# A GEGLU and Fourier-mixing kernel: moving the side work, stream requests and bank fills of a seven-product matrix multiplication

## The chip, the cores and the metric

The kernel runs on one core of a Trainium2 chip. The metric is the device time of one execution in microseconds (us). A time is given as the median of three runs with the lowest and the highest of them. Engine names are those of the profile: PE is TensorE (matrix products), PEld its weight loads, DVE is VectorE, ACT is ScalarE, POOL is GpSimd, SP is SyncE. POOL and SP here only start DMA transfers.

## The reference

The input is 2048 tokens of 640 numbers, all in fp32. One branch is a Fourier mixing by two dense matrices, the other a gated feed-forward layer with 1728 hidden numbers; a sigmoid gate per token mixes them.

```python
def _A_ref(x, dft_seq_re, dft_seq_im, dft_hid_re, dft_hid_im):
    a = jnp.einsum("bsd,ed->bse", x, dft_hid_re)
    b = jnp.einsum("bsd,ed->bse", x, dft_hid_im)
    y = jnp.einsum("ts,bse->bte", dft_seq_re, a) - jnp.einsum("ts,bse->bte", dft_seq_im, b)
    return y

def _B_ref(x, w_gate, w_up, w_down):
    return (_gelu(x @ w_gate) * (x @ w_up)) @ w_down

g = _sigmoid((x * gate_w).sum(-1, keepdims=True))
return g * a + (1 - g) * b
```

## The kernel before

**Numbers.** [...] One product is three matmuls into the same PSUM bank (`mm3`, L101 to L103): high by high, high by low, low by high. A high part is a copy on ACT (L82), a low part a difference on DVE (L85), so DVE's low part always waits for ACT's high part. A bank holds 128 x 512 fp32 and there are eight banks.

**Stages.** First the tokens and the first weights are loaded and summed; then the loop over hidden blocks `for f in range(1, NF)` (L1353, NF = 13) computes gate and up projections; behind it, from some 366 us of the span on, come the Fourier mixing and the down projection.

**The hidden-block loop.** Each f is a block of 128 hidden numbers; the tokens are two pairs, tp 0 and 1. `gate_up` (L596) makes one f for one token pair by a Strassen-Winograd form: seven block products instead of eight, with sums of weight blocks on the left (S1 to S4) and sums of token blocks on the right (T1 to T4). Bank X takes A11, then S2 T2, then S3 T3, then u5 x1, each added to what is there. So between them the running value must be taken out of X: the sum into s1 (L629, DVE), the copy s2 (L149, ACT), the sum into s5 (L667, DVE). Bank Z takes S1 T1, then D and S4. `gate_up` is a generator; its pieces are the steps 0 to 6 (rows) of the loop below, each taken for tp 0 and then tp 1.

From f = 3 on (PAIRED) blocks go in couples: the first of a couple (3, 5, 7, 9, 11) also computes products shared by both blocks, again by seven products, in `together` and `together_up`. From f = 5 on (THIRD) there is a third such product, S1 times T1 of two blocks and two token pairs, in `together_s` (L554). Its parts:

- The right operands T1, T2, T3 are streams: made once in f = 4 by `sums_across` (its functions `s123`, with loads `loads_s` ahead of them), stored in DRAM, and fetched again for each couple by `load_across` (L1319; the transfer is L1321 on POOL's queue) into tiles `xs`. T4 (`s4th`) stays on the core.
- The left operands are weight sums in tiles `wt` (`make_third`, L260). They are loaded and summed in the second block of the couple before.
- The results for the couple's second block f + 1 are parked in tiles `sz` (L579 and L588 are the last sums into them) and put back into two fresh banks pZ by `unpark` (L591, the ACT copies L594).

The other streams of a couple, `xq` and `xu`, go by the same `load_across`. Results of a block go to DRAM with `keep` (L448, POOL): `hA` four times a block, as soon as DVE has made them, and `hT` for some blocks. The wait of a store holds up whatever stands behind it in POOL's queue.

**Weights.** `load_w` (L213) and `load_up` (L228) ask for a block's weights on SP (tiles `wa`, `wb`, `wq`, `wu`); `make_w` (L290) and `make_up` give back lists of small sums, high and low parts with a cost each. In the list, `ws` are S1 to S4 of one block, `wd` is D, `wq` holds the left sums shared by a couple.

**What sets the order.** The loop stands in `in_order(PE, ACT, DVE, POOL)` (L1352): on these engines instructions run in the order in which they are written. SP's requests go in their queue's order, each when its tile is free. The lists of small sums are put into one queue, `fills`, at the start of an f; `fill` (L1326) takes from its head whenever PE work has been written, in proportion to that work, and all that is left is written at the end of the f. So the list's order decides which sums stand ahead of which other DVE and ACT work.

In a block the loop reads:

```python
for step in range(8 if not kind else 7):
    if third and step == 6:
        unpark(f + 1, zs, parks)
    for tp, w in enumerate(work):
        run(w)
```

`kind` is 1 for the first of a couple, 2 for the second, 0 before the couples; `third` is true for first blocks from f = 5 on. After the rows of a step come the requests that the diff shows.

Of the kernel before, what the change touches and what calls it, by code (L numbers as in the profile page):

```python
# [9 lines left out]
F32 = mybir.dt.float32  # L10
F32R = mybir.dt.float32r
# [3 lines left out]
P = 128  # L15
# [7 lines left out]
NF = F // P  # L23
# [5 lines left out]
PAIRED = 3  # L29
THIRD = 5  # L30
# [7 lines left out]
def kernel(  # L38
# [36 lines left out]
    def mtile(dt, name):  # L75
        return pool.tile([P, T], dt, tag="m", name=name, bufs=15)
# [4 lines left out]
    def high(hi, raw):  # L81
        nc.scalar.activation(hi, raw, AF.Copy)  # L82
# [120 lines left out]
    def wsmall(dt, name):  # L203
        return pool.tile([P, 2, P], dt, tag="w", name=name, bufs=6)

    def pair_of(f):


        return 0 if f < PAIRED or f >= NF else 2 - (f - PAIRED + 1) % 2
# [3 lines left out]
    def load_w(f):  # L213


        if f >= NF:
            return
        ra, rb = slot(F32, [P, 8, P], f"wa{f}r"), wsmall(F32, f"wb{f}")
        nc.sync.dma_start(ra, wf[f - 1, :, :8])
        nc.sync.dma_start(rb, wf[f - 1, :, 8:])  # L220
        rq = None
        if pair_of(f) == 1:
            rq = slot(F32, [P, 8, P], f"wq{f}r")
            nc.sync.dma_start(rq[:, 0:2], wf[f, :, 0:2])
            nc.sync.dma_start(rq[:, 2], wf[f, :, 4])
        wraw[f] = ra, rb, rq
# [30 lines left out]

        return W, [(112, across), (0, high_u), (78, low_u)]

    def make_third(f):  # L260

        W = {}
        raw, own = ([mtile(dt, f"wt{f}{n}").rearrange("p (b c) -> p b c", c=P) for n in names] for dt, names in ((F32, "ab"), (F32R, "hl")))
        last = wsmall(F32R, f"wt{f}")
        a, b = raw
        for v, c in ((a, 8), (b, 2)):
            for q in range(2):
                nc.sync.dma_start(v[:, 2 * q : 2 * q + 2], wf[f - q, :, c : c + 2])

        def sums():  # L270
            tt(a, a, b, op=ALU.add)
            high(last[:, 0], a[:, 1])

        def across():
            tt(b[:, 0], a[:, 0], a[:, 1], op=ALU.add)
            tt(b[:, 2], a[:, 2], a[:, 0], op=ALU.subtract)
            tt(b[:, 1], b[:, 0], a[:, 2], op=ALU.subtract)
            tt(b[:, 3], a[:, 3], b[:, 1], op=ALU.subtract)
            high(own[0], b)

        def lows():
            low(last[:, 0], last[:, 1], a[:, 1])
            low(*own, b)
            W["A22p"] = last[:, 0], last[:, 1]
            for k in range(4):
                W[f"S{k + 1}p"] = at(own, k)

        return W, [(69, sums), (112, across), (97, lows)]

    def make_w(f):  # L290

# [187 lines left out]
    hid, todo = {}, deque()  # L479
# [624 lines left out]
    W0, load_part, parts, first_strassen = load_first()  # L1104
    Bs = []
    B, tiles, load, piece, tsum, his, lows = load_x(0)
# [28 lines left out]
    with in_order(ACT, DVE, PE):  # L1135
# [5 lines left out]
        for d in range(ND):  # L1141
# [3 lines left out]
            if d == 0:  # L1145
                a, b = halves
# [37 lines left out]
        B, tiles, load, piece, tsum, his, lows = load_x(1)  # L1184
# [62 lines left out]
        W, work = make_w(1)  # L1247
        sums, high_a, sums2, high_c, low_a, diff, low_c = (do for _, do in work)
# [103 lines left out]
    with in_order(PE, ACT, DVE, POOL):  # L1352
        for f in range(1, NF):  # L1353
            kind = pair_of(f)
            if f == PAIRED:
                loadu()
                fills.extend([*t4, *u123[:3], *late_work, *u123[3:], *u4])
            fills.extend(todo)
            todo.clear()
            if kind == 1:  # L1360
                up, work = make_up(f, load_up(f))
                fills.extend(work)
            if f == PAIRED - 1:
                loadp()
                fills.extend(t123)
            if f == THIRD - 1:
                loads_s()
                fills.extend(s123)
            if f + 1 < NF:
                nxt, work = make_w(f + 1)  # L1370
                if kind != 1 or f == PAIRED:
                    fills.extend(work)
            if kind == 1 and f > PAIRED:
                fills.extend(work)
            if pair_of(f + 1) == 1 and f + 1 >= THIRD:
                ws, work = make_third(f + 1)
                fills.extend(work)
            if f == NF - 1:
                for k in range(2):
                    fetch_xn(k)  # L1380
                    load_c(k)

                def made():
                    sums_made.pop(0)()

                for k in range(2):
                    fills.extend([(126, partial(split_xa, k)), (122, made), (245, partial(split_c, k))])
                fills.extend([(126, partial(split_xa, 2)), (122, made)])
            state.update(pe=0, done=0, all=sum(c for c, _ in fills), pe_all=2450 if not kind else (2994, 1768)[kind - 1] if f < THIRD else (3198, 1496)[kind - 1])
            s5 = pair(F32, f"s5{f}")  # L1390
            xs = {}
            work = [gate_up(f, W, Bs[tp], tp, s5[:, tp], s1t, xs, s4, zs) for tp in range(2)]
            more = together(f, W, Tp, s1t, xs) if kind == 1 else iter(())
            more_up = together_up(f, W, up, s4) if kind == 1 else iter(())
            store_left()
            if f == 2:
                k = len(fills) // 2
                rest = [fills.pop() for _ in range(len(fills) - k)]
                fills.extend([*sum_h0(0), *sum_h0(1), *reversed(rest)])
                state["all"] = sum(c for c, _ in fills)  # L1400
            third = kind == 1 and f >= THIRD
            if third:
                parks.clear()
                more_s = together_s(f, W, ws, s5, zs, parks)
            for k in range(4):
                run(more)
                if third and k in (1, 3):
                    load_across(f, "xs", Ts, kepts, k)
            for step in range(8 if not kind else 7):
                if third and step == 6:  # L1410
                    unpark(f + 1, zs, parks)
                for tp, w in enumerate(work):
                    run(w)
                    if third:
                        if step == 0:
                            run(more_s if not tp else more)
                        if (step, tp) == (0, 1):
                            load_across(f, "xu", Tu, keptu, 1)
                            run(more_s)
                            load_across(f, "xu", Tu, keptu, 2)  # L1420
                            run(more)
                            run(more_s)
                            run(more)
                            run(more_s)
                            load_across(f, "xu", Tu, keptu, 3)
                        elif (step, tp) == (2, 0):
                            run(more_s)
                            run(more_s)
                        elif (step, tp) == (3, 0):
                            run(more_s)  # L1430
                    elif (step, tp) in ((0, 1), (1, 1)):
                        run(more)
                        if step == 0:
                            run(more)
                    if (2, 0) < (step, tp) < (6, 0):
                        run(more_up)
                if step < 2 and kind == 1 and PAIRED < f < THIRD:
                    for k in ((1,), (2, 3))[step]:
                        load_across(f, "xu", Tu, keptu, k)
                if step == 4 and pair_of(f + 1) == 1 and f + 1 > PAIRED:  # L1440
                    for k in (1, 2, 3):
                        load_across(f + 1, "xq", Tp, keptp, k)
                if step == 6 and pair_of(f + 1) == 1 and f + 1 >= THIRD:
                    load_across(f + 1, "xs", Ts, kepts, 2)
                if step == 5 and f == THIRD - 1:
                    for _, do in s4th:
                        do()
                if step == 5:
                    load_w(f + 2)
                if f == NF - 1 and step == 3:  # L1450
                    fetch_xn(2)
                if f == NF - 1 and step == 5:
                    load_c(2)
                    fetch_xn(3)
            for v in (more, more_up) + ((more_s,) if third else ()):
                next(v, None)
            while fills:
                fills.popleft()[1]()
            W = nxt
# [59 lines left out]
    for i, (j, ri, b, sp) in enumerate(cseq):  # L1519
# [31 lines left out]
        n = f"{j}{ri}"  # L1551
# [358 lines left out]
```

## Time and profile before

| | us |
|---|---|
| median of 3 runs | 1039.74 (1038.99 to 1040.75) |
| the profiled execution's own time | 1040.26 |
| its span (first to last instruction) | 1038.5 |
| DVE busy in the span | 838.8 (81%) |
| ACT busy in the span | 510.6 (49%) |

The profile is of one execution. Busy time is the time in which an engine runs an instruction. A row of a timeline reads: start in us from the span's start, duration, engine, line, operation, output tile <- input tiles (buffer numbers left out), shape; in square brackets how long the engine had stood idle just before and what ended that. A row of a group of waits reads: who waited <- for whom, then total us, times, longest us. The end of a matmul is modelled, so the idle time that stands beside one is a little short of what a wait really costs.

### The profile page before, as it was taken

The page shows a single profiled execution, that of the slowest core. Times are in us where ns is not written, and L with a number is a line of the kernel's source. Part 1 is how long each engine was busy: PE and PEld are TensorE (multiplying, and loading weights), DVE is VectorE, ACT ScalarE, POOL GpSimd, SP SyncE. Part 2 cuts the span into 40 slices and gives each one's busy share as a digit, 9 for nine tenths or more (in the row PEclk, how much of TensorE's full clock was granted, in tenths as well). Part 3 has the DMA queues.
Part 4 walks back from the last instruction along what each step waited for, and adds up shares of the span by engine and source line. Part 5 has one row for each costly group of instructions (what it writes and reads, how often), then busy time and mean ns, then how long its engine had stood idle before and what let it go on. Part 6 is the DMA issues. An engine that isn't in the chain of part 4 may idle for free.

```text
span 1038.5 us, 13424 instructions
## 1 busy us (share of the span) xinstructions
PE 1018.9 (98%) x4477; PEld 834.6 (80%) x4477; DVE 838.8 (81%) x1197; ACT 510.6 (49%) x666; POOL 188.5 (18%) x330
## 2 busy tenths in 40 slices
PE   9999989999999999999999999999999999999998
PEld 7888767777777878888888888888888888888887
DVE  8987783859584798986978697769798997997796
ACT  6644453545454575442444344334636737655340
POOL 1221230323130011023103310310111010111112
PEclk9999998999999999999999999999999999999999
DMA  9466674676666898679768976989989998997856
GB/s 352 150 218 216 216 244 158 218 241 216 233 218 228 275 285 215 208 266 392 256 204 305 395 241 199 358 306 302 330 315 359 351 393 332 349 372 219 264 161 92
DMA packets 98598, 276.51 MB, mean 266 GB/s; under 512 B 13088, under 2 KB 25504, under 8 KB 98528
## 3 DMA queue, kind: packets, MB, share of 16 engines
q1 hardware_dynamic: 69216, 182.88, 50.4%
q0 software_dynamic: 29024, 92.57, 28.1%
q8 instruction: 35, 0.57, 0.2%
q14 instruction: 35, 0.29, 0.1%
q10 hardware_dynamic: 288, 0.20, 0.1%
HBM read 201.13 MB, written 66.60 MB: 258 GB/s over the span
## 4 chain that ended last, share of the span: by engine, by line
PE 88%; DVE 4%; issue 3%; DMA 2%; ACT 1%; POOL 1%; POOLq 0%; DVEq 0%; ACTq 0%
PE pX L103 5%; PE pX L102 5%; PE pX L101 5%; PE pZ L101 3%; PE pZ L102 3%; PE pZ L103 3%; PE pL L102 3%; PE pL L103 3%; PE pL L101 3%; DMA xs<-xs 2%; PE pV L102 2%; PE pV L103 2%; PE pV L101 2%; PE pY L102 1%; PE pR L102 1%
## 5 line engine op out<-in xcount | busy, mean ns | idle before, releaser
L82 ACT ACTIVATE ch<-csa 128x1024 fp32r<-128x1024 f32 x32 | 34.0, 1062 | 79.2 <-DVE csa L886 67.0
L448 POOL DMA_DIRECT2D hA<-s x48 | 26.1, 545 | 175.2 <-DVE s L679 154.6
L82 ACT ACTIVATE ch<-cra 128x1024 fp32r<-128x1024 f32 x32 | 33.9, 1059 | 45.3 <-DVE cl L85 14.3
L85 DVE TENSOR_TENSOR cl<-cra,ch 128x1024 fp32r<-128x1024 f32 x32 | 39.1, 1222 | 18.5 <-ACT ch L82 16.3
L85 DVE TENSOR_TENSOR cl<-crb,ch 128x1024 fp32r<-128x1024 f32 x32 | 39.1, 1223 | 14.8 <-ACT ch L82 14.7
L102 PE MATMUL pL<-cl,xah 128*128 128x512 f32 x128 | 49.8, 389 | 0.0
L103 PE MATMUL pL<-ch,xal 128*128 128x512 f32 x128 | 49.8, 389 | 0.0
L101 PE MATMUL pL<-ch,xah 128*128 128x512 f32 x128 | 48.8, 389 | 0.0
L82 ACT ACTIVATE ch<-crb 128x1024 fp32r<-128x1024 f32 x32 | 33.8, 1056 | 28.4 <-DVE cl L85 10.8
L85 DVE TENSOR_TENSOR cl<-csa,ch 128x1024 fp32r<-128x1024 f32 x32 | 39.1, 1222 | 9.3 <-ACT ch L82 8.2
L85 DVE TENSOR_TENSOR cl<-csb,ch 128x1024 fp32r<-128x1024 f32 x32 | 39.2, 1225 | 4.2 <-ACT ch L82 3.2
L82 ACT ACTIVATE ch<-csb 128x1024 fp32r<-128x1024 f32 x32 | 34.0, 1062 | 12.8 <-DVE csb L889 4.6
L149 ACT ACTIVATE s<-pX 128x512 f32<-128x512 f32 x41 | 23.9, 593 | 32.8 <-PE pX L103 32.1
L1510 POOL DMA_DIRECT2D uA<-c x8 | 4.3, 540 | 168.9 <-DVE c L1622 168.3
L102 PEld LDWEIGHTS pL<-cl,xah 128*128 128x128 f32 x128 | 24.0, 188 | 5.0
L101 PEld LDWEIGHTS pL<-ch,xah 128*128 128x128 f32 x128 | 24.0, 188 | 5.0
L103 PEld LDWEIGHTS pL<-ch,xal 128*128 128x128 f32 x128 | 24.0, 188 | 5.0
L82 ACT ACTIVATE kh<-kw 128x1024 fp32r<-128x1024 f32 x24 | 25.5, 1063 | 5.0 <-PE kL L102 3.1
L667 DVE TENSOR_TENSOR s<-s,pX 128x512 f32<-128x512 f32 x24 | 16.3, 684 | 13.9 <-PE pX L103 13.9
L102 PE MATMUL pX<-cl,xah 128*128 128x512 f32 x64 | 25.0, 391 | 0.7 <-DVE cl L85 0.7
L85 DVE TENSOR_TENSOR kl<-kw,kh 128x1024 fp32r<-128x1024 f32 x18 | 22.0, 1222 | 4.4 <-ACT kh L82 4.4
L103 PE MATMUL pX<-ch,xal 128*128 128x512 f32 x64 | 25.0, 391 | 0.0
(3785 smaller groups left out, 3519.9 us busy)
## 6 DMA issues: line engine op xcount, KB each, us to landing
cra<-in_ct SPq DMA_DIRECT2D x64, 512.0 KB, 5.2
crb<-in_ct SPq DMA_DIRECT2D x64, 512.0 KB, 5.9
kr<-hA SPq DMA_DIRECT2D x36, 512.0 KB, 7.8
hA<-s POOLq DMA_DIRECT2D x48, 256.0 KB, 3.1
ux<-uA SPq DMA_DIRECT2D x24, 512.0 KB, 7.8
ux<-uT SPq DMA_DIRECT2D x16, 512.0 KB, 6.4
hT<-s POOLq DMA_DIRECT2D x24, 256.0 KB, 4.6
xq<-xp POOLq DMA_DIRECT2D x12, 512.0 KB, 5.2
```

What stands on the lines that cost most here:

```text
L82: nc.scalar.activation(hi, raw, AF.Copy)
L85: nc.vector.tensor_tensor(lo, raw, hi.bitcast(F32), op=ALU.subtract)
L101: nc.tensor.matmul(ps, lh, rh, start=first, stop=False, skip_group_check=True)
L102: nc.tensor.matmul(ps, lh, rl, start=False, stop=False, skip_group_check=True)
L103: nc.tensor.matmul(ps, ll, rh, start=False, stop=last, skip_group_check=True)
L149: nc.scalar.activation(m, src, AF.Copy)
L448: nc.gpsimd.dma_start(to[:, i], src)
L667: tt(s5, s5, X, op=ALU.add)
L1510: nc.gpsimd.dma_start(to[:, i], src)
```

## The change

Five things move; no product is added or removed.

- `make_third` is split: `load_third(f)` asks for the raw weights one block earlier, and the sums, high parts and low parts of `wt` are woven into the head of the list of f's second block: first the sums, after two sums of `make_w` the differences, and so on, instead of at the end of the list.
- T2 of the next couple is asked for after step 5, not step 6, which puts the request ahead of the four `hA` stores.
- `unpark` comes ahead of step 5, not 6.
- `loads_s` and the first three functions of `s123` move from the start of f = 4 to step 4 of f = 3; `s4th` is put off to f = 5's side work.
- In the first block of a couple from f = 5 on, the weights of the second block are asked for and summed from step 1 of that block, not from step 5 of the block before.

```diff
--- before.py
+++ after.py
@@ -257,25 +257,33 @@
 
         return W, [(112, across), (0, high_u), (78, low_u)]
 
-    def make_third(f):
-
-        W = {}
-        raw, own = ([mtile(dt, f"wt{f}{n}").rearrange("p (b c) -> p b c", c=P) for n in names] for dt, names in ((F32, "ab"), (F32R, "hl")))
-        last = wsmall(F32R, f"wt{f}")
-        a, b = raw
+    traw = {}
+
+    def load_third(f):
+
+        traw[f] = a, b = [mtile(F32, f"wt{f}{n}").rearrange("p (b c) -> p b c", c=P) for n in "ab"]
         for v, c in ((a, 8), (b, 2)):
             for q in range(2):
                 nc.sync.dma_start(v[:, 2 * q : 2 * q + 2], wf[f - q, :, c : c + 2])
 
+    def make_third(f):
+
+        W = {}
+        a, b = traw.pop(f)
+        own = [mtile(F32R, f"wt{f}{n}").rearrange("p (b c) -> p b c", c=P) for n in "hl"]
+        last = wsmall(F32R, f"wt{f}")
+
         def sums():
             tt(a, a, b, op=ALU.add)
-            high(last[:, 0], a[:, 1])
 
         def across():
             tt(b[:, 0], a[:, 0], a[:, 1], op=ALU.add)
             tt(b[:, 2], a[:, 2], a[:, 0], op=ALU.subtract)
             tt(b[:, 1], b[:, 0], a[:, 2], op=ALU.subtract)
             tt(b[:, 3], a[:, 3], b[:, 1], op=ALU.subtract)
+
+        def highs():
+            high(last[:, 0], a[:, 1])
             high(own[0], b)
 
         def lows():
@@ -285,7 +293,7 @@
             for k in range(4):
                 W[f"S{k + 1}p"] = at(own, k)
 
-        return W, [(69, sums), (112, across), (97, lows)]
+        return W, [(69, sums), (112, across), (0, highs), (97, lows)]
 
     def make_w(f):
 
@@ -1364,16 +1372,16 @@
                 loadp()
                 fills.extend(t123)
             if f == THIRD - 1:
-                loads_s()
-                fills.extend(s123)
-            if f + 1 < NF:
+                fills.extend(s123[3:])
+            third = kind == 1 and f >= THIRD
+            if f + 1 < NF and not third:
                 nxt, work = make_w(f + 1)
+                if pair_of(f + 1) == 1 and f + 1 >= THIRD:
+                    ws, (sums, across, highs, lows) = make_third(f + 1)
+                    work = [sums, *work[:2], across, *work[2:4], highs, work[4], lows, *work[5:]]
                 if kind != 1 or f == PAIRED:
                     fills.extend(work)
-            if kind == 1 and f > PAIRED:
-                fills.extend(work)
-            if pair_of(f + 1) == 1 and f + 1 >= THIRD:
-                ws, work = make_third(f + 1)
+            if kind == 1 and PAIRED < f < THIRD:
                 fills.extend(work)
             if f == NF - 1:
                 for k in range(2):
@@ -1398,7 +1406,6 @@
                 rest = [fills.pop() for _ in range(len(fills) - k)]
                 fills.extend([*sum_h0(0), *sum_h0(1), *reversed(rest)])
                 state["all"] = sum(c for c, _ in fills)
-            third = kind == 1 and f >= THIRD
             if third:
                 parks.clear()
                 more_s = together_s(f, W, ws, s5, zs, parks)
@@ -1407,7 +1414,7 @@
                 if third and k in (1, 3):
                     load_across(f, "xs", Ts, kepts, k)
             for step in range(8 if not kind else 7):
-                if third and step == 6:
+                if third and step == 5:
                     unpark(f + 1, zs, parks)
                 for tp, w in enumerate(work):
                     run(w)
@@ -1440,12 +1447,21 @@
                 if step == 4 and pair_of(f + 1) == 1 and f + 1 > PAIRED:
                     for k in (1, 2, 3):
                         load_across(f + 1, "xq", Tp, keptp, k)
-                if step == 6 and pair_of(f + 1) == 1 and f + 1 >= THIRD:
+                if step == 5 and pair_of(f + 1) == 1 and f + 1 >= THIRD:
                     load_across(f + 1, "xs", Ts, kepts, 2)
-                if step == 5 and f == THIRD - 1:
-                    for _, do in s4th:
-                        do()
-                if step == 5:
+                if f == THIRD - 2 and step == 4:
+                    loads_s()
+                    fills.extend(s123[:3])
+                if f == THIRD - 1 and step == 5:
+                    todo.extend(s4th)
+                if step == 5 and THIRD <= f + 2 < NF and pair_of(f + 2) == 1:
+                    load_third(f + 2)
+                if third and step == 1:
+                    load_w(f + 1)
+                    nxt, parts = make_w(f + 1)
+                    fills.extend(parts)
+                    state["all"] += sum(c for c, _ in parts)
+                if step == 5 and not (f + 2 >= THIRD and pair_of(f + 2) == 2):
                     load_w(f + 2)
                 if f == NF - 1 and step == 3:
                     fetch_xn(2)
```

Lines behind `make_third` stand 8 higher in the changed kernel: L667 becomes L675, L629 L637, L448 L456, L1321 L1329.

Three places show how the order moves. The first is POOL's queue at the end of f = 6, before the change: the three `xq` streams and `xs72` (T2) for f = 7, the stores `hA` of f = 6, and `hT`.

```order
L1321 DMA xq73_1830<-xp3_569 128x1024
L448 DMA hA02_67<-s26_0_1797 128x512
L448 DMA hA02_67<-s1510_1563 128x512
L448 DMA hA12_73<-s26_1_1810 128x512
L448 DMA hA12_73<-s1511_1479 128x512
L1321 DMA xs72_1866<-xs2_574 128x1024
L448 DMA hT02_79<-s25_0_1582 128x512
L448 DMA hT02_79<-s55_1461 128x512
```

After it:

```order
L1329 DMA xq73_1830<-xp3_569 128x1024
L1329 DMA xs72_1846<-xs2_574 128x1024
L456 DMA hA02_67<-s26_0_1794 128x512
L456 DMA hA02_67<-s1510_1551 128x512
L456 DMA hA12_73<-s26_1_1804 128x512
L456 DMA hA12_73<-s1511_1471 128x512
L456 DMA hT02_79<-s25_0_1578 128x512
L456 DMA hT02_79<-s55_1455 128x512
```

The request for `xs72` has moved past the four stores of f = 6, to stand right behind the last `xq`.

The second place is DVE in f = 6, the twelve instructions that end in the sum L667 into s5 of the first token pair (`s56` from bank `pX6_0`), before:

```order
L85 TENSOR_TENSOR wd7_1784<-wb7_1686,wd7_1784 128x128
L85 TENSOR_TENSOR ws7l_1782<-ws7r_1762,ws7h_1781 128x1024
L271 TENSOR_TENSOR wt7a_1716<-wt7a_1716,wt7b_1717 128x512
L275 TENSOR_TENSOR wt7b_1717<-wt7a_1716 128x128
L276 TENSOR_TENSOR wt7b_1717<-wt7a_1716 128x128
L277 TENSOR_TENSOR wt7b_1717<-wt7b_1717,wt7a_1716 128x128
L278 TENSOR_TENSOR wt7b_1717<-wt7a_1716,wt7b_1717 128x128
L659 TENSOR_TENSOR s26_0_1797<-s26_0_1797,pZ6_0_1692 128x512
L85 TENSOR_TENSOR wt7_1720<-wt7a_1716,wt7_1720 128x128
L85 TENSOR_TENSOR wt7l_1719<-wt7b_1717,wt7h_1718 128x512
L659 TENSOR_TENSOR s26_1_1810<-s26_1_1810,pZ6_1_1693 128x512
L667 TENSOR_TENSOR s56_1725<-s56_1725,pX6_0_1741 128x512
```

After it:

```order
L85 TENSOR_TENSOR wt7l_1723<-wt7b_1690,wt7h_1722 128x512
L311 TENSOR_TENSOR ws7r_1784<-wb7_1696,wa7r_1695 128x256
L312 TENSOR_TENSOR ws7r_1784<-wa7r_1695,wb7_1696 128x256
L85 TENSOR_TENSOR wq7l_1782<-wq7r_1699,wq7h_1781 128x896
L316 TENSOR_TENSOR ws7r_1784<-ws7r_1784,wa7r_1695 128x256
L317 TENSOR_TENSOR ws7r_1784<-wa7r_1695,ws7r_1784 128x256
L330 TENSOR_TENSOR wb7_1696<-wa7r_1695 128x128
L85 TENSOR_TENSOR wd7_1812<-wb7_1696,wd7_1812 128x128
L667 TENSOR_TENSOR s26_0_1794<-s26_0_1794,pZ6_0_1660 128x512
L85 TENSOR_TENSOR ws7l_1810<-ws7r_1784,ws7h_1809 128x1024
L667 TENSOR_TENSOR s26_1_1804<-s26_1_1804,pZ6_1_1661 128x512
L675 TENSOR_TENSOR s56_1725<-s56_1725,pX6_0_1738 128x512
```

The `wt7` sums have gone from here to the front of the block (between row 234 and 247) and the `ws7` and `wq7` work has taken their place; the sum into `s56` is the 258th row in both. On ACT the same piece of f = 6, with the copies L149 of s2 out of `pX6_0` and `pX6_1`, before:

```order
L82 ACTIVATE wq7h_1759<-wq7r_1689 128x896
L82 ACTIVATE ws7h_1781<-ws7r_1762 128x1024
L82 ACTIVATE wd7_1784<-wb7_1686 128x128
L82 ACTIVATE wt7_1720<-wt7a_1716 128x128
L149 ACTIVATE s26_0_1797<-pX6_0_1741 128x512
L82 ACTIVATE wt7h_1718<-wt7b_1717 128x512
L149 ACTIVATE s26_1_1810<-pX6_1_1752 128x512
```

After it:

```order
L82 ACTIVATE wt7_1724<-wt7a_1689 128x128
L82 ACTIVATE wt7h_1722<-wt7b_1690 128x512
L82 ACTIVATE wq7h_1781<-wq7r_1699 128x896
L149 ACTIVATE s26_0_1794<-pX6_0_1738 128x512
L149 ACTIVATE s26_1_1804<-pX6_1_1754 128x512
L82 ACTIVATE ws7h_1809<-ws7r_1784 128x1024
L82 ACTIVATE wd7_1812<-wb7_1696 128x128
```

Both copies now stand ahead of the high parts of `ws7` and `wd7`.

The third place is DVE at the end of f = 3 and the start of f = 4, from the low part `ws4l` on; `xst1`, `xs12` to `xs22` are the stream sums of `s123`. Before:

```order
L85 TENSOR_TENSOR ws4l_1205<-ws4r_1166,ws4h_1204 128x1024
L543 TENSOR_TENSOR s4311_1169<-s4311_1169,pH3u_1148 128x512
L672 TENSOR_TENSOR s23_0_1134<-s23_0_1134,pZ3_0_1043 128x512
L547 TENSOR_TENSOR s4301_1196<-s4301_1196,pZ3u_1149 128x512
L672 TENSOR_TENSOR s23_1_1146<-s23_1_1146,pZ3_1_1052 128x512
L679 TENSOR_TENSOR s23_0_1134<-s23_0_1134,s53_1001 128x512
L683 TENSOR_TENSOR s4300_1179<-s4300_1179,pX3_0_1042 128x512
L684 TENSOR_TENSOR s1300_1033<-s1300_1033,s4300_1179 128x512
L679 TENSOR_TENSOR s23_1_1146<-s23_1_1146,s53_1001 128x512
L683 TENSOR_TENSOR s4301_1196<-s4301_1196,pX3_1_1051 128x512
L684 TENSOR_TENSOR s1301_1040<-s1301_1040,s4301_1196 128x512
L1290 TENSOR_TENSOR xst1_1287<-xs12_1263,xs11_1261 128x512
```

After it:

```order
L85 TENSOR_TENSOR ws4l_1205<-ws4r_1166,ws4h_1204 128x1024
L551 TENSOR_TENSOR s4311_1169<-s4311_1169,pH3u_1148 128x512
L1298 TENSOR_TENSOR xst1_1227<-xs12_1215,xs11_1213 128x512
L1299 TENSOR_TENSOR xs12_1215<-xs22_1217,xs12_1215 128x512
L680 TENSOR_TENSOR s23_0_1134<-s23_0_1134,pZ3_0_1043 128x512
L85 TENSOR_TENSOR xs1_1235<-xst1_1227,xs1_1235 128x512
L555 TENSOR_TENSOR s4301_1196<-s4301_1196,pZ3u_1149 128x512
L1302 TENSOR_TENSOR xs22_1217<-xs22_1217,xst1_1227 128x512
L1303 TENSOR_TENSOR xs21_1219<-xs21_1219,xs22_1217 128x512
L680 TENSOR_TENSOR s23_1_1146<-s23_1_1146,pZ3_1_1052 128x512
L687 TENSOR_TENSOR s23_0_1134<-s23_0_1134,s53_1001 128x512
L691 TENSOR_TENSOR s4300_1179<-s4300_1179,pX3_0_1042 128x512
```

The stream sums, which began behind the last sums of f = 3, now stand between them.

## Prediction

> **What bounds the kernel now.** The page comes first: how busy the engines are and which of them stand in the chain that ended last.
>
> ```profile
> span 1038.5 us, 13424 instructions
> ...
> PE 1018.9 (98%) x4477; PEld 834.6 (80%) x4477; DVE 838.8 (81%) x1197; ACT 510.6 (49%) x666; POOL 188.5 (18%) x330
> ...
> PE 88%; DVE 4%; issue 3%; DMA 2%; ACT 1%; POOL 1%; POOLq 0%; DVEq 0%; ACTq 0%
> ```
>
> TensorE is busy for 1018.9 of 1038.5 us. So 19.6 us of idle time is all that a reordering can win, apart from matmuls that run below full clock. The next view splits the span into stretches (length; busy time and instructions of PE, its weight loads, DVE, ACT, POOL; granted clock; share of the DMA engines; GB/s). 111 to 366 is the part of the hidden-block loop from f=4 on, with the wait for f=5's T2 cut out as 155 to 163, and 366 to 786 lies behind the loop.
>
> ```profile
> 111.00:155.00 44.00, 39.64 (x169) 30.98 (x168) 34.98 (x68) 22.30 (x38) 12.31 (x22) 1.00 0.69 217
> 155.00:163.00 8.00, 5.09 (x13) 4.07 (x14) 1.48 (x4) 1.08 (x2) 0.54 (x1) 0.57 0.83 298
> 163.00:366.00 203.00, 195.32 (x841) 156.01 (x840) 139.28 (x252) 98.46 (x162) 43.84 (x79) 1.00 0.67 222
> 366.00:786.00 420.00, 419.27 (x1850) 346.69 (x1848) 353.73 (x463) 198.73 (x224) 72.87 (x132) 1.00 0.83 286
> ```
>
> The first three stretches hold 4.36, 2.91 and 7.68 us of PE idle time, 14.95 of the 19.6. The last holds 0.73: there 1850 matmuls start 420/1850 = 0.227 us apart, so what the loop gains is passed on to the end. What PE waits for from 100 to 380 us (total, times, longest):
>
> ```profile
> PE pH5s L101 <- DMA xs<-xs: 4.3, 1, 4.3
> PE pX L101 <- ACT s L149: 3.4, 3, 1.6
> PE pX L101 <- DVE s L667: 2.9, 2, 2.4
> PE pZ L101 <- ACT pZ L594: 1.5, 4, 0.4
> PE pH9s L101 <- DMA xs<-xs: 1.2, 1, 1.2
> ...
> PE pH7s L101 <- DMA xs<-xs: 0.7, 1, 0.7
> PE pH11s L101 <- DMA xs<-xs: 0.7, 1, 0.7
> ```
>
> The rows on xs are the waits for T2, by f. L149 is the copy of s2 out of bank X and L594 the put-back of the parked banks: both belong to f=6, 8, 10 (L594 to 12 too). L667 belongs to f=4.
>
> **What a wait costs.** Three rows of f=7, the last matmul before the wait, the one that waits, and the next:
>
> ```profile
> 210.11 0.39 PE L103 MATMUL pH7t<-xq,wq7l 128*128 128x512 f32 x1
> ...
> 211.21 0.47 PE L101 MATMUL pH7s<-xs,wt7h 128*128 128x512 f32 x1 [0.71 <-DMA xs<-xs]
> 211.52 0.39 PE L102 MATMUL pH7s<-xs,wt7h 128*128 128x512 f32 x1
> ```
>
> From 210.11 to 211.52 are 1.41 us for two steps, which without the wait take 2 x 0.227 = 0.45. The loss is 0.96: the shown 0.71 and 0.25 more, as the idle time counts only from the modelled end of the matmul ahead. Each wait below is priced at its row plus 0.25.
>
> **Part 1, f=5's T2: 6.7 us.**
>
> ```profile
> 153.23 0.39 PE L103 MATMUL pH5t<-xq,wq5l 128*128 128x512 f32 x1
> ...
> 157.91 0.77 PE L101 MATMUL pH5s<-xs,wt5h 128*128 128x512 f32 x1 [4.29 <-DMA xs<-xs]
> ...
> 162.67 0.39 PE L103 MATMUL pZ<-xT01h,ws5l 128*128 128x512 f32 x1
> ```
>
> From the first to the third row are twelve starts in 9.44 us; at 12 x 0.227 = 2.72 they lose 6.7. Of these 4.45 are the late start; the other 2.3 come from the clock, 0.57 in that stretch. When was T2 asked for? Two pieces from the chain of waits (start, duration), and the third xq request of POOL in f=4 and in f=6:
>
> ```profile
> 152.26 5.52 DMA xs<-xs
> 206.27 4.80 DMA xs<-xs
> ```
>
> ```profile
> 141.78 0.54 POOL L1321 DMA_DIRECT2D xq<-xp  x1 [3.79 <-DVE wt5b L276]
> ```
>
> ```profile
> 196.76 0.54 POOL L1321 DMA_DIRECT2D xq<-xp  x1 [0.70 <-DVE wt7a L271]
> ```
>
> T2 goes out behind four hA stores, which wait for DVE. After the change it stands right behind the third xq, so it goes out at about 142.4 and 197.4, which is 9.9 and 8.9 us sooner. At 5.52 us to landing it is there by 147.9 in f=5 (the matmul could start at 153.23 + 0.23 = 153.46) and by 202.9 in f=7 (needed at 210.34). More traffic beside it may delay it by 5 us and still cost nothing. If this cover were gone, the whole term would come back (the third rival). The s123 sums make T2 of f=5; half of them move up to f=3, so they are no later. I take all of it, 6.7; the ends are 0 and 6.7.
>
> **Part 2, T2 of f=7, 9 and 11: 3.4 us.** 0.7 + 1.2 + 0.7 + 3 x 0.25 = 3.35, by the same argument; the ends are 0 and 3.4.
>
> **Part 3, f=4: 1.4 us.** The matmul that waits, and DVE's idle time ahead of its sums:
>
> ```profile
> 142.90 0.50 PE L101 MATMUL pX<-x05h,wa 128*128 128x512 f32 x1 [2.41 <-DVE s L667]
> ```
>
> ```profile
> 122.17 0.69 DVE L672 TENSOR_TENSOR s<-s,pZ 128x512 f32<-128x512 f32 x1 [0.51 <-PE pZ L103]
> ...
> 135.96 1.09 DVE L85 TENSOR_TENSOR wq5l<-wq5r,wq5h 128x896 fp32r<-128x896 f32 x1 [1.62 <-ACT wq5h L82]
> ...
> 139.16 0.29 DVE L85 TENSOR_TENSOR wd<-wb,wd 128x128 fp32r<-128x128 f32 x1 [1.12 <-ACT wd L82]
> ```
>
> PE loses 2.9 + 2 x 0.25 = 3.4 here and waits for DVE, which from 119 us on stands still in these three places alone. The new order holds the same sums up to the second L667, only permuted (the third order excerpt has a piece). The stream sums now fill the hole of 0.51, and other sums stand between wq5h and wq5l, so 1.62 should shrink or go; wd's low half still follows its high half, so 1.12 stays. DVE thus comes 0.5 to 2.1 us sooner; as 1.62 is a wait for ACT alone, I take two thirds of the larger end, 1.4. The ends are 0 (a new wait in their place; L629 now stands behind the xs lows and may hold S2 T2) and 3.4.
>
> **Part 4, f=6, 8 and 10: 0.3 us.** With the put-back at step 5 and ACT's copies of s2 ahead of ws7h, the waits for ACT go: 3.4 + 3 x 0.38 + 6 x 0.25 = 6.0. But do they come back as a wait for DVE?
>
> ```profile
> 194.60 0.29 DVE L85 TENSOR_TENSOR wd<-wb,wd 128x128 fp32r<-128x128 f32 x1 [1.12 <-ACT wd L82]
> ...
> 199.63 0.68 DVE L667 TENSOR_TENSOR s<-s,pX 128x512 f32<-128x512 f32 x1
> ```
>
> ```profile
> 200.42 0.45 PE L101 MATMUL pX<-x05h,wa 128*128 128x512 f32 x1
> ```
>
> In both orders DVE has the same 26 instructions from L692 of f=5, second pair (L700 after) to this L667 of f=6 (L675 after), only permuted. The 1.12 at wd is its one idle place on this way, and wd's low half still follows its high half. So L667 still ends at 200.3, and the u5 x1 matmul, which adds to bank X only after it, still starts at 200.42: PE gets to that point sooner and waits there. DVE becomes the bound in the middle of these blocks. I take 0.1 for each; the ends are 0 and 6.0.
>
> **Part 5, f=12: 0.3 us.** The put-back's 0.38 + 0.25 goes; the ends are 0 and 0.6, and I take half.
>
> **Parts at nothing.** The weights' load and sums moved into f = 5, 7, 9, 11 are the same instructions; splitting make_third adds none. Their cover is the second rival and the last.
>
> **Sum.** 6.7 + 3.4 + 1.4 + 0.3 + 0.3 = 12.1 us. The profiled execution took 1040.26 us (its span of 1038.5 and 1.76 around it), 0.52 above the median of 1039.74. So 1028.2 for such an execution, and **1027.6** for the median.
>
> **Rivals.** *DVE does not take part 4 back*: for it speaks that 1.12 of DVE's idle time per block is a wait for ACT, which a freer ACT could shorten. The gain is then 12.1 + 5.7 + 0.3 = 18.1: 1021.6. Against it stands that DVE has the same work before the same sum.
>
> *The next streams become late.* T1 and T3 aren't asked for sooner than DVE lets the hA stores go, while PE comes to them sooner.
>
> ```profile
> 164.96 0.39 PE L101 MATMUL pZ<-xs,wt5h 128*128 128x512 f32 x1
> ```
>
> T1 of f=5 is used here. Without part 1 that is at 164.96 - 6.7 = 158.3. It was the second xs request, just behind 152.26, and now is the first, so it has 6.0 us; the streams took 4.8 and 5.5. The margin is half a us. If T1 comes as late in all four blocks as T2 did in f=7, it costs 4 x 0.95 = 3.8: the gain is 8.3, the time 1031.4.
>
> [...]
>
> *T2 still waits.* The trace of before doesn't show when T2's buffer comes free. If that is as late as the hA stores, parts 1 and 2 fall away and the change doesn't do what it says: a gain of 2.0, 1037.7.
>
> *Slower: weights late.* wa8r is now asked for in row 1 of f=7, behind wu7r, in a buffer that the last matmul on wq7l frees, just ahead of the first row here:
>
> ```profile
> 216.06 0.39 PE L101 MATMUL pZ<-xs,wt7h 128*128 128x512 f32 x1
> ...
> 222.96 0.40 PE L101 MATMUL pH7s<-xT11h,wt 128*128 128x512 f32 x1
> ```
>
> ```profile
> 219.04 0.42 DVE L303 TENSOR_TENSOR ws8r<-wb,wa8r 128x256 f32<-128x256 f32 x1 [0.44 <-PE pH7s L103]
> 219.38 0.42 DVE L304 TENSOR_TENSOR ws8r<-wa8r,wb 128x256 f32<-128x256 f32 x1
> 219.71 0.68 DVE L579 TENSOR_TENSOR sz<-sz,pH7s 128x512 f32<-128x512 f32 x1
> ```
>
> ```profile
> wa8r<-in_wf SPq DMA_DIRECT2D x1, 512.0 KB, 3.4
> ...
> wa12r<-in_wf SPq DMA_DIRECT2D x1, 512.0 KB, 7.2
> ```
>
> Behind the two sums on wa8r DVE has L579, which must have read bank H before the matmul at 222.96. L579 ends 1.35 us after the first sum starts, so PE is held from a start at 221.6 on, a landing of 5.3 us after the buffer is free at 216.3. wa8r took 3.4, but wa12r 7.2. At 12 us, in f=7 and f=9, each costs 6.7 + 0.25 and 2.3 for the clock as in part 1: 18.5, a net loss of 6.4 and 1046.1. It turns to a loss from about 9 us to landing.
>
> **How the numbers follow.** The forecast has 0.60, as parts 1 and 2 rest on margins of 5 us; its own range is 1025.6 to 1029.6 (part 3 at 3.4; parts 3 to 5 at nothing). The others have: late streams 0.18; DVE not taking it back 0.14; T2 still waiting 0.05; weights late 0.03. The range reaches over the first three, from 1021.5 to 1033 (1031.4, and 1.4 more where part 3 gives nothing). A measurement of this kernel can tell about 0.2%, 2.1 us, from no change. Faster by more: 0.60 + 0.18 + 0.14 = 0.92; within: 0.05; slower: 0.03.
>
> **What would show it.** Right: no wait of pH5s, pH7s, pH9s, pH11s for xs and no stretch at 0.57 of the clock; T2's request right behind the third xq; in f=6 and 8 no wait for the put-back or the copy of s2, but in their place one for the L667 sum (now L675), about as long in all. Wrong: waits of pZ for xs (late T1), of DVE's first sum on wa8r with PE behind it, or f=6, 8 and 10 shorter by some us (DVE not taking it back).

## The result, and the profile after

Six runs of the changed kernel have a median of 1033.31 us (1031.1 to 1036.54), beside 1040.58 us (1038.99 to 1043.02, six runs) for the kernel before. The ratio is 0.9928, with a 95% interval of 0.9907 to 0.995: faster by 0.7%, which is 7.3 us where 12.1 were forecast, and 0.3 us outside the upper end of the range. That miss of the range is smaller than the 0.84 us by which the six runs of before lie above the three on record (1039.74), so the gain, 7.3 for 12.1, says more than the range. The profiled execution is the fastest of the six, at 1031.1 us: 9.2 less than the profiled execution of before. Two runs of one experiment, T2 alone, were disturbed (1268.26 and 3413.74 us) and are left out of its median.

The page of the changed kernel, the lines that answer to those of before:

```profile
span 1029.3 us, 13418 instructions
...
PE 1014.8 (99%) x4477; PEld 832.8 (81%) x4477; DVE 837.2 (81%) x1197; ACT 511.8 (50%) x666; POOL 188.9 (18%) x330
...
PE 81%; issue 10%; DVE 4%; POOL 3%; DMA 1%; ACT 0%; POOLq 0%; SPq 0%; DVEq 0%; ACTq 0%
```

PE's idle time fell from 19.6 to 14.5 us; its busy time fell too, from 1018.9 to 1014.8, mostly because the matmuls behind f=5's T2 no longer run at a low clock (0.57 before, 1.00 now): before, the 52 us from 111 to 163 held 44.7 us of busy time for 182 matmuls; now the 44 us from 111 to 155 hold 42.3 for as many. What PE waits for from 90 to 375 us of the changed kernel:

```profile
PE pX L101 <- DVE s L675: 4.4, 3, 1.7
PE pX L101 <- DVE s L637: 2.2, 3, 1.6
PE pH9s L101 <- DVE sz L587: 1.6, 1, 1.6
PE pH7s L101 <- DVE sz L587: 1.3, 1, 1.3
PE pX L102 <- DVE cl L85: 0.7, 1, 0.7
```

Not one row on xs is left, and none on the put-back or the copy of s2. In their place stand L675, as forecast, and two rows that the forecast had only in its least likely rival: the wait for L587, the sum into the parked result. No row of pZ on xs came either, so PE doesn't wait for T1 either: that the profiled 1031.1 us lie beside the 1031.4 of the late-streams rival is chance. T2 of f=5 now goes out at 142.49, where the forecast had about 142.4:

```profile
142.49 0.54 POOL L1329 DMA_DIRECT2D xs<-xs  x1 [1.08 <-PE pZ L103]
```

The stretches that answer to the four of before (length; busy time and instructions of PE, its weight loads, DVE, ACT and POOL; granted clock; share of the DMA engines; GB/s):

```profile
111.00:147.50 36.50, 34.82 (x149) 27.35 (x148) 30.51 (x59) 19.71 (x34) 9.95 (x18) 1.00 0.74 234
147.50:155.00 7.50, 7.50 (x34) 6.15 (x34) 4.06 (x9) 2.87 (x5) 3.48 (x7) 1.00 0.80 292
155.00:357.00 202.00, 193.89 (x841) 156.84 (x840) 140.49 (x256) 100.90 (x163) 43.45 (x78) 1.00 0.69 230
357.00:777.00 420.00, 419.27 (x1849) 346.50 (x1847) 353.52 (x463) 198.98 (x224) 72.95 (x132) 1.00 0.83 286
```

The stretch with f=5's T2 holds 34 matmuls in 7.5 us and no idle time, at full clock. The stretch behind it holds 8.1 us of idle time, where before had 7.7 with the three smaller T2 waits in it. The 420 us behind the loop are the same.

Where the new wait comes from, in DVE's timeline of f=7 (start, duration, line, tiles, idle time and its end) and in PE's of f=7 and f=9:

```profile
213.71 0.43 DVE L311 TENSOR_TENSOR ws8r<-wb,wa8r 128x256 f32<-128x256 f32 x1 [2.60 <-DMA wa8r<-in_wf]
214.05 0.42 DVE L312 TENSOR_TENSOR ws8r<-wa8r,wb 128x256 f32<-128x256 f32 x1
214.38 0.68 DVE L587 TENSOR_TENSOR sz<-sz,pH7s 128x512 f32<-128x512 f32 x1
```

```profile
215.12 0.50 PE L101 MATMUL pH7s<-xT11h,wt 128*128 128x512 f32 x1 [1.30 <-DVE sz L587]
...
266.79 0.50 PE L101 MATMUL pH9s<-xT11h,wt 128*128 128x512 f32 x1 [1.65 <-DVE sz L587]
```

And the transfers that DVE waited for (size, us to landing), with the stretch from wa8r's request to its landing:

```profile
wa8r<-in_wf SPq DMA_DIRECT2D x1, 512.0 KB, 6.6
...
wa10r<-in_wf SPq DMA_DIRECT2D x1, 512.0 KB, 6.9
```

```profile
206.90:213.50 6.60, 6.60 (x31) 5.29 (x29) 1.12 (x2) 3.62 (x6) 1.10 (x2) 1.00 1.00 387
```

DVE stands at the first sum on wa8r for 2.60 us and behind it stands L587, which PE needs. The transfer took 6.6 us instead of the 3.4 of before; during it the mean share of the DMA engines was 1.00. In f=9 it is the same with wa10r: DVE's first sum on it starts at 265.37, 0.2 us after the landing, though the profile puts DVE's wait there, 2.94 us, down to a stream, xu.

### The profile page after: what moved, and what is told of

Same layout as the page of the kernel before. It is cut to its first block, busy times and chain, and to the rows that moved or that the text cites. A ratio compares the mean times of both kernels' runs of the same rounds, so it can differ in the third digit from the quotient of the medians.

```text
span 1029.3 us, 13418 instructions
## 1 busy us (share of the span) xinstructions
PE 1014.8 (99%) x4477; PEld 832.8 (81%) x4477; DVE 837.2 (81%) x1197; ACT 511.8 (50%) x666; POOL 188.9 (18%) x330
## 4 chain that ended last, share of the span: by engine, by line
PE 81%; issue 10%; DVE 4%; POOL 3%; DMA 1%; ACT 0%; POOLq 0%; SPq 0%; DVEq 0%; ACTq 0%
PE pX L102 5%; PE pX L103 5%; PE pX L101 5%; PE pL L103 3%; PE pL L102 3%; PE pL L101 3%; PE pZ L103 3%; PE pZ L101 3%; PE pZ L102 3%; PE pV L103 2%; PE pV L102 2%; PE pV L101 2%; PE pY L103 1%; PE pR L103 1%; PE pQ L103 1%
## 5 line engine op out<-in xcount | busy, mean ns | idle before, releaser
L456 POOL DMA_DIRECT2D hA<-s x48 | 26.2, 546 | 165.8 <-DVE s L687 145.4
L149 ACT ACTIVATE s<-pX 128x512 f32<-128x512 f32 x41 | 24.1, 596 | 37.4 <-PE pX L103 36.8
L675 DVE TENSOR_TENSOR s<-s,pX 128x512 f32<-128x512 f32 x24 | 16.1, 682 | 13.0 <-PE pX L103 13.0
L681 ACT ACTIVATE s<-s 128x512 f32<-128x512 f32 x16 | 10.1, 634 | 30.3 <-DVE s L680 30.3
```

Source lines behind the costliest of these rows:

```text
L149: nc.scalar.activation(m, src, AF.Copy)
L456: nc.gpsimd.dma_start(to[:, i], src)
L675: tt(s5, s5, X, op=ALU.add)
L681: nc.scalar.activation(s2, s2, AF.Gelu_apprx_tanh)
```

## The experiments

All are timed beside the kernel before, on the same chip within a group; ratios are to it. The first four ran beside a median of 1038.83 us (17 runs).

**The changed kernel again.** No edit.

> The changed kernel once more, for its spread and a second profile. Theory (weights late): in f=7 and f=9 PE waits for the sum L587 behind wa8r and wa10r, 1.3 to 1.7 us each or more, and the runs above 1033 us are those in which these waits are longer and the clock falls (granted clock 0.998 or less). Expected: median 1032 to 1034, lowest about 1031, waits of pH7s and pH9s on L587 again. Rival (noise of the whole kernel, as before's own runs go from 1039.0 to 1043.0): slow runs at an unchanged clock.

1033.41 us (1033.1 to 1034.81), ratio 0.9943 (0.9927 to 0.9959); four of five runs at a clock of 0.998. Its profile has the same waits as above but for f=7: pH7s waits 2.09 us, as wa8r took 7.4 us. This time the clock gives way behind the wait, to 0.68 (windows, then PE's timeline):

```profile
213.00:217.00 4.00, 1.91 (x7) 1.23 (x6) 2.38 (x7) 1.13 (x3) 0.00 (x0) 0.89 0.10 39
217.00:221.00 4.00, 4.00 (x14) 3.15 (x14) 1.23 (x2) 2.37 (x5) 0.00 (x0) 0.68 0.41 120
```

```profile
215.64 0.50 PE L101 MATMUL pH7s<-xT11h,wt 128*128 128x512 f32 x1 [2.09 <-DVE sz L587]
215.98 0.49 PE L102 MATMUL pH7s<-xT11l,wt 128*128 128x512 f32 x1
216.28 0.63 PE L103 MATMUL pH7s<-xT11h,wt 128*128 128x512 f32 x1
216.70 0.63 PE L101 MATMUL pZ7u<-xu,wu7h 128*128 128x512 f32 x1
...
219.26 0.53 PE L101 MATMUL pV7u<-xT04h,wa7h 128*128 128x512 f32 x1
```

From 216.28 on seven matmuls start some 0.43 us apart instead of 0.23. With the longer wait (0.8) this makes the 2.3 us between this execution and the profiled one above. So the theory held, and this profile shows the clock at 0.68 behind the L587 wait. Of the eleven runs of both groups, the three below 1033 us have a clock of 1.0 and seven of the eight above it one of 0.997 or 0.998; the eighth, at 1033.67 us, has 1.0, so the clock isn't all of the spread.

**Weights early again.** The request goes back to the block before; the sums stay where the change put them.

```diff
                 if third and step == 1:
-                    load_w(f + 1)
                     nxt, parts = make_w(f + 1)
...
-                if step == 5 and not (f + 2 >= THIRD and pair_of(f + 2) == 2):
+                if step == 5:
                     load_w(f + 2)
```

> Only the request for the second block's weights goes back to step 5 of the block before; all else as changed. Theory (weights late): the waits of pH7s and pH9s on L587 are gone, wa8r lands in 3.4 to 3.6 us, the profiled execution takes 1031.1 - (1.30 + 1.65 + 2 x 0.25) = 1027.7, near the recorded forecast of 1027.6 for the median, and the spread shrinks, clock 1.0 in all. Rival (the requests were moved because T2 or wu would suffer): a wait on xs or wu of 1 us or more appears in f=7 or 9 and the time stays at 1031 or above.

1028.42 us (1027.91 to 1029.4), ratio 0.9894 (0.9876 to 0.9912), all runs at a clock of 1.0, and waits only on L675 (4.4) and L637 (2.3) in the loop. That is a gain of 10.4 us beside this group's before, and 12.1 between the profiled executions (1040.26 and 1028.16), which is the forecast's sum. wa8r was asked for at 191.7 instead of 206.9 and then took 7.9 us, not the 3.4 to 3.6 expected; as nothing waits for it that early, that is harmless. So the old place doesn't promise the old landing time either. The late request cost 1033.41 - 1028.42 = 5.0 us.

**T2 late again.**

```diff
-                if step == 5 and pair_of(f + 1) == 1 and f + 1 >= THIRD:
+                if step == 6 and pair_of(f + 1) == 1 and f + 1 >= THIRD:
                     load_across(f + 1, "xs", Ts, kepts, 2)
```

> Only the request for T2 goes back behind the hA stores (after step 6); all else as changed. Parts 1 and 2 of the forecast say that this request alone is worth 10.1 us: waits on xs of pH5s, pH7s, pH9s, pH11s return, as PE now also comes sooner to T2 by what the side work gained: pH5s 3.5 to 4.5 us with a slow clock behind it, pH7s and pH9s 1 to 4, so 1041 to 1046. Rival (T2 was late because of the other transfers, not of its place in the queue): waits of under 1 us, time within 3 us of the changed kernel.

1037.29 us (1035.1 to 1042.28, 12 runs), ratio 0.9993 (0.9976 to 1.001): 3.9 us slower than the changed kernel, not 8 to 13. The waits returned, but smaller:

```profile
PE pH11s L101 <- DMA xs<-xs: 1.7, 1, 1.7
...
PE pH5s L101 <- DMA xs<-xs: 1.3, 1, 1.3
...
PE pH9s L101 <- DMA xs<-xs: 0.6, 1, 0.6
PE pH7s L101 <- DMA xs<-xs: 0.3, 1, 0.3
```

Both expectations missed in size. POOL shows why for f=5:

```profile
148.71 0.54 POOL L456 DMA_DIRECT2D hA<-s  x1 [0.72 <-DVE s L692]
149.26 1.74 POOL L1329 DMA_DIRECT2D xs<-xs  x3
```

T2 still goes out behind the last hA store, but this store now starts at 148.71 instead of 151.56: DVE gets to the h results sooner in the new order. T2 starts 3.0 us sooner than before the change, and PE could use it only 1.2 us sooner (152.30 instead of 153.46). So the rest of the change takes away part of the same wait; the two gains don't add.

**The put-back late again.**

```diff
-                if third and step == 5:
+                if third and step == 6:
                     unpark(f + 1, zs, parks)
```

> Only the put-back goes back to step 6; all else as changed. The forecast has DVE as the bound in f=6, 8 and 10, so the put-back's wait returns (0.4 to 0.5 us at pZ in f=6, 8, 10, 12) but the wait on the sum L675 shrinks by about the same in f=6 and 8: at most 1 us slower than the changed kernel on the same chip. Rival (the put-back was on the path): 4 x 0.63 = 2.5 us slower.

1033.88 us (1032.12 to 1034.78), ratio 0.9943 (0.9925 to 0.9962), 0.5 us above the changed kernel, which is within the spread of both. The put-back's wait is back (1.5 us in four pieces), the waits on L637 in f=6 and 8 are gone in turn. DVE is the bound there; the earlier put-back is worth little.

The next four ran beside a median of 1039.6 us (13 runs).

**T2 alone.** The kernel before, with one digit changed:

```diff
-                if step == 6 and pair_of(f + 1) == 1 and f + 1 >= THIRD:
+                if step == 5 and pair_of(f + 1) == 1 and f + 1 >= THIRD:
                     load_across(f + 1, "xs", Ts, kepts, 2)
```

> The kernel before with one edit: T2 asked for after step 5 instead of 6. Theory: in the kernel before, T2's place behind the hA stores caused the four waits on xs alone, so this edit is worth parts 1 and 2, 10.1 us, by itself: about 1030 in the profile where before takes 1040, ratio 0.990, ahead of the whole change (0.993 to 0.994), because the weights are still asked for early and the waits on L587 (then L579) don't come. Waits left: L667 in f=4 (2.4), the put-back and the copies of s2. Rival (from the run with T2 late: only 3.9 us hang on T2's place): ratio 0.996 and new waits on xs T1 or elsewhere.

> The kernel before with T2 asked for sooner, once more, for a profile at full speed. It took 1033.7, a gain of 5.9 where parts 1 and 2 have 10.1. Theory (T2 gone, something next is late): no wait on xs T2, but new waits in f=5, 7 or 9 on T1 or T3 (xs), on wu or on copies, 3 to 4 us in sum, or a clock below 1.0. Rival: T2 still waits in part (pH5s on xs, 2 us or more).

1033.5 us (six runs, 1031.94 to 1034.01; ratio 0.9944, 0.9926 to 0.9962) and, in the second group, 1033.36 us beside 1039.75 (ratio 0.994, 0.9918 to 0.9962). The waits, in the profile of the second group's execution of 1031.24 us at a clock of 1.0:

```profile
PE pX L101 <- ACT s L149: 3.4, 3, 1.6
PE pX L101 <- DVE s L667: 2.9, 2, 2.4
PE pZ L101 <- ACT pZ L594: 1.5, 4, 0.4
PE pX L102 <- DVE cl L85: 0.7, 1, 0.7
PE pX L103 <- DMA xal<-xn: 0.2, 1, 0.2
```

This is before's list without the T2 rows, to the tenth, plus 0.2 for xal behind the loop. Between profiled executions the edit is worth 1040.26 - 1031.24 = 9.0 of the 10.1 us. Of what was expected to eat up the gain, no new wait came and only the lower clock did: the other three runs of this group are at 0.998 and 1033.2 to 1033.6 us. So the clock falls in most runs, at a cost of about 2.2 us (one run of the first group took 1033.68 us at a clock of 1.0, so it isn't all of the loss); that it does so behind the 2.4 us wait on L667 in f=4 is the author's guess, as that wait is the longest left; no run shows it. One moved request thus gives the same median as the whole change.

**Weights and their sums later still.**

```diff
-                if third and step == 1:
+                if third and step == 2:
                     load_w(f + 1)
                     nxt, parts = make_w(f + 1)
```

> The changed kernel with load and sums of the second block's weights put off from step 1 to step 2 of f=5, 7, 9, 11. Theory: the harm in f=7 and 9 is that the weight sums stand in DVE's queue ahead of the park sum L587 while wa8r is on its way; asked for later still, but with the sums behind L587, they hold up nothing: the L587 waits go, 0.4 us of wu waits may come, and the time falls by about 2.5 to 3 against the changed kernel (ratio about 0.991). Rival (the weights are simply late): still later, it gets slower than the changed kernel, ratio 0.995 or above, with waits in f=8.

1028.89 us (1028.53 to 1030.37), ratio 0.9906 (0.9887 to 0.9925); the L587 waits are gone, and no new wait in f=8 came. The harm isn't the late transfer as such: it is that the sums which wait for it stand in DVE's queue ahead of a sum that PE needs.

**All right sums in f=4.**

```diff
-                fills.extend(s123[3:])
+                loads_s()
+                fills.extend(s123)
...
-                if f == THIRD - 2 and step == 4:
-                    loads_s()
-                    fills.extend(s123[:3])
```

> The changed kernel with loads_s and all of s123 back at the start of f=4. Part 3 of the forecast: the earlier sums are worth 1.4 us. Rival: the sums only trade one wait for another (L637 of 1.6 us at S2 T2 goes, a wait of about 1.7 on L675 comes), no difference within 0.3 us; part 3's gain then belongs to the weaving of the wt sums.

1032.65 us (1031.4 to 1033.77), ratio 0.9939 (0.992 to 0.9959): no slower than the changed kernel. The rival held: the L637 wait of 1.6 us in f=4 goes and one of 1.8 on L675 comes, so 1.4 of the 3.4 us that f=4 lost before stay won without the earlier right sums.

**A slower pace.** With weights early as above, and in f=6, 8, 10 and 12:

```diff
-        while fills and not (some and not fills[0][0]) and state["done"] <= 1.25 * state["all"] * state["pe"] / state["pe_all"]:
+        while fills and not (some and not fills[0][0]) and state["done"] <= (0.8 if state["pe_all"] == 1496 else 1.25) * state["all"] * state["pe"] / state["pe_all"]:
```

> The changed kernel with the weights asked for early (as in the run before) and, in f=6, 8, 10 and 12, the side work handed out at 0.8 instead of 1.25 times PE's progress, so that fewer small sums stand ahead of L637 and L675. Theory of the forecast (DVE's order bounds these blocks, not its total work): waits on L637 and L675 in f=6, 8, 10 shrink from 1.7 + 1.7 + 1.0 + 0.3 + 0.3 to about 0.4 each, so 3 to 4 us less than with weights early alone: about 1024.5 where that took 1028.4. Rival (DVE's total work bounds them): the waits move to the start of f=7, 9, 11 (copies into bank V, T1 asked for late) and the time stays at 1028.

1024.09 us (1022.94 to 1025.38), ratio 0.9854 (0.9831 to 0.9877): 4.3 us below weights early (timed in the other group, at 0.9894; between the two profiled executions 2.8), the fastest of all, 1.5% below the kernel before. What is left in the loop:

```profile
PE pZ L101 <- DMA xs<-xs: 1.8, 2, 1.2
PE pX L101 <- DVE s L637: 1.6, 1, 1.6
PE pX L101 <- DVE s L675: 1.0, 3, 0.3
```

L675 fell from 4.4 to 1.0 and L637 keeps only f=4's 1.6. In f=6 the last two `ws7` sums, the low part of `wd`, for which DVE waited 1.12 us for ACT with the weaving at the old pace, and `ws7l` now stand behind L675 of the first token pair. So it was the order on DVE that bound f=6, 8 and 10, not its total work. The first row is the forecast's other rival: T1, asked for behind the hA stores, is now late for a faster PE, in f=7 and f=9.

**Left sums last.** Weights early, and the wt sums at the end of the list. It ran beside 1039.75 us (17 runs).

```diff
-                    work = [sums, *work[:2], across, *work[2:4], highs, work[4], lows, *work[5:]]
+                    work = [*work, sums, across, highs, lows]
```

> The changed kernel with the weights asked for early (1028.4) and with the wt sums back at the end of the side work's list. Theory: the weaving is what part 3 and the rest of the gain over T2 alone hang on; with the wt sums last DVE reaches L675 later: waits on L675 of 4.1, 4.1 and 2.8 us in f=6, 8 and 10, 1034 to 1036. Rival (part 4 as forecast: the order of the sums ahead of L675 doesn't matter, since they are the same 26 instructions): within 1 us of 1028.4.

1041.03 us (1038.36 to 1042.0), ratio 1.0015 (1.0003 to 1.0026): 12.6 us slower than with the weaving, all runs at a clock of 0.992 to 0.995.

```profile
PE pX L101 <- DVE s L675: 10.6, 3, 3.9
```

The waits are the expected ones within 0.3 us (3.89, 3.88, 2.78). Against the 4.4 us on L675 with the weaving that is 6.2 more. The time missed the expected 1034 to 1036 because that left out the clock: behind the three waits it is 0.50, 0.50 and 0.57 for 4 us, and at the 2.3 us that the forecast read for such a fall in f=5, three of them, an estimated 6.9, are enough for the other 6. The rival fell: the same sums in another order do matter. No more of them stand ahead of L675 than with the weaving, but DVE now waits for ACT in two more places, as in f=6:

```profile
190.43 0.68 DVE L667 TENSOR_TENSOR s<-s,pZ 128x512 f32<-128x512 f32 x1
192.52 0.29 DVE L85 TENSOR_TENSOR wt<-wt7a,wt 128x128 fp32r<-128x128 f32 x1 [1.41 <-ACT wt L82]
193.04 0.69 DVE L85 TENSOR_TENSOR wt7l<-wt7b,wt7h 128x512 fp32r<-128x512 f32 x1 [0.23 <-ACT wt7h L82]
```

On ACT the high parts of `wt7` stand behind two activations that wait for this L667. The 1.6 us are most of the 2.2 by which the wait in f=6 grew; with the weaving the one idle place on this way is the 1.12 us at wd, as the forecast said.

## Why the forecast was wrong: point by point

- **T2's waits, 10.1 us (parts 1 and 2).** Right: all four are gone, and so is the low clock in f=5 (0.57 before, 1.00 now); T2 alone gave 9.0 between profiled executions. But the forecast read the wait as T2's place in POOL's queue alone. Taking that back in the new order costs only 3.9, because there the hA stores go sooner as well.
- **f=4, 1.4 us (part 3).** Right in size: 3.4 us of loss became 1.56 + 0.25 = 1.8, on L637, the sum that the forecast named as the possible new wait. Of its reasons one held and one didn't. The idle time of 1.62 us at wq5l is gone, and L667 of the first token pair (now L675) ends 1.7 us sooner (at 141.2 instead of 142.9). But the stream sums in the idle 0.51 us brought a new idle 1.22 us, for ACT, ahead of L637, and the earlier right sums gain 0.25 us at most (all right sums in f=4). The gain hangs on the weaving of the wt sums: without it f=4 waits 1.57 us on L637 and 0.73 on L149 (left sums last), which with 0.25 for each is 2.8 of the old 3.4.
- **f=6, 8, 10, 0.3 us (part 4).** Right: L675 with 4.4 and L637 with 0.6, five waits in all, are 5.0 + 1.25 = 6.3, where the old waits lost 6.0. DVE took it back. It is the order on DVE that does it: at the slower pace the waits on L675 and L637 fall from 6.7 to 2.6 us.
- **f=12, 0.3 us.** The put-back's wait is gone, 0.6.
- **The weights, costed at nothing.** This is the step that failed. The forecast had the mechanism, with L587 as the sum that is held and 5.3 us to landing as the point from which PE is held, but took wa8r's 3.4 us from before as what it would still take, put the term at nothing and gave the case 0.03. The 7.2 us of wa12r stood beside that 3.4 in the forecast; by its own point they mean 1.9 us of waiting a block. In the run wa8r took 6.6 us, 1.3 beyond that point, and PE waited 1.30; wa10r took 6.9, 1.6 beyond, and PE waited 1.65. In the second profile 7.4 gave 2.09. Each wait follows from the landing; only the landing was mis-sized. It was read where wa8r was asked for in the old order, a stretch with the DMA engines at a share of 0.57:

```profile
200.30:203.80 3.50, 3.46 (x16) 2.51 (x15) 3.09 (x6) 1.24 (x3) 0.63 (x2) 1.00 0.57 186
```

  In the new order the request falls among the T1, T3 and xu streams and the hT stores, at a share of 1.00. The forecast gave T2 a margin of 5 us for more traffic beside it, and no wait for T2 came; for the weights it took over the 3.4 us, and wa8r then took 6.6 at 1.00 where it had taken 3.4 at 0.57. But the share alone doesn't set the landing: the 7.2 us of wa12r before fall into a stretch at 0.67,

```profile
297.50:304.70 7.20, 6.99 (x30) 4.87 (x29) 6.71 (x15) 4.34 (x9) 0.55 (x1) 1.00 0.67 231
```

  and wa8r took 7.4 us at 0.89 in the second profile and 7.9 at 0.83 with weights early. That wa8r landed late and that PE waited for it is shown; what sets the length of one landing stays open.
- **The sum.** In the profiled execution 10.1 + 1.6 - 0.3 + 0.6 - (1.30 + 1.65 + 0.50) = 8.6, measured 9.2. The median lies 2.2 above that execution, which is the fastest. In three of the six runs the clock is 0.997 or 0.998, and the second profile shows it at 0.68 behind the wait in f=7; but the runs at 1.0 go up to 1032.7 too, so the clock is part of it; the forecast had a price for that, but only at 6.7 us of waiting. With the request put back the median is 1028.42, 0.8 above the forecast's 1027.6: without the weights' term the forecast's sum stands, though its smaller terms missed both ways and cancel by luck (1.6 - 0.3 + 0.6 where it had 1.4 + 0.3 + 0.3).

## What to carry to other kernels

A moved request did not keep its old landing time here: wa8r took 3.4 us in its old place, 6.6 to 7.4 in the new one, and 7.9 in the old place once the requests around it had moved. Price a moved request by the longest landing that the trace has for a transfer of its size, and ask what waits if it takes that long. In a queue that runs in written order, ask for each instruction that waits on a transfer what stands behind it; putting the weight sums behind the one sum that PE needed won as much as asking earlier. And when side work shares an engine with sums on the path, handing it out more slowly can be worth a few us: 4.3 here by the medians, for one factor.

## What the runs showed of the hardware

TensorE's clock fell behind waits far shorter than the 4.29 us of before: to 0.68 behind 2.09 us in the second profile of the changed kernel, and to 0.67 behind 1.80 us with all right sums in f=4 (the first row below, right behind that wait). But it stayed at 1.00 behind 1.73 us in f=6 of the first profile of the changed kernel, behind 2.41 us in f=4 of T2 alone, and behind 2.55 us in f=9 with T2 late (the second row). So in these profiles, between some 1.8 and 2.55 us, the length of a wait doesn't decide whether the clock falls.

```profile
145.00:149.00 4.00, 4.00 (x14) 3.17 (x13) 3.93 (x7) 1.79 (x4) 1.72 (x4) 0.67 0.80 303
```

```profile
272.00:276.00 4.00, 4.00 (x19) 3.26 (x18) 1.83 (x4) 3.29 (x7) 0.00 (x0) 1.00 0.39 127
```

The same kernel falls to 0.998 in some runs and not in others, about 2 us apart: T2 alone, in its second group, took 1031.24 us at 1.0 and 1033.2 to 1033.59 at 0.998. No run shows what decides it.
